# Output stores that go by the less used of two queues, in chunked attention with a token-mixing MLP on one core

## The chip, the core and the metric

The kernel runs on one core of a Trainium2 chip. The metric is device microseconds (us) of one execution; lower is better. Five engines matter: TensorE (PE in the profile: matrix products and transposes), VectorE (DVE), ScalarE (ACT), GpSimd (POOL) and SyncE (SP). SyncE computes nothing: it issues DMA transfers. GpSimd can compute, but here it mostly issues transfers too. The two issue them by different queues, which the profile calls q1, hardware_dynamic (SyncE) and q0, software_dynamic (GpSimd). Both queues feed the same 16 DMA engines of the core.

## The reference

Chunked softmax attention over 8 batches, 8 heads, 576 positions, 64 features, in chunks of 64 positions; then a mixing MLP over the positions of each batch. Cut to what matters:

```python
# attention, each chunk of 64 positions by itself
scores = scale * q_c @ k_c.T
attn = softmax(scores)
out = attn @ v_c                          # then laid out as x[B, S, 512]
# token mixing, per batch
wq = x @ w_q                              # [576, 64]
wk = x @ w_k
W_tok = (1 / sqrt(64)) * wq @ wk.T        # [576, 576]
mixed = W_tok @ x                         # [576, 512]
return relu(mixed) @ w_out                # float32, [8, 576, 512]
```

The output is 8 x 576 x 512 floats, 9.44 MB. It is written to memory once.

## The kernel before, in words

The work is cut into 20 units: for each of the 8 batches two blocks of 256 positions (`m` 0 and 1), and the last 64 positions of the batches, joined in pairs (`m` None). Each unit goes through attention (`attention`), the projections (`project`) and, once a batch has all of its units, the mixing (`mixing`, `mix_out`). W_tok is not formed: the kernel multiplies wk by x first.

The order of all steps is a list written by hand, `ORDER`. A word names a step, an engine (P, V, S for TensorE, VectorE, ScalarE) and a PSUM bank. `Graph.write` walks through it and emits each step. So every engine's instructions, and those of both queues, stand in a fixed order, and an instruction that waits holds up those behind it on its engine.

Loads go by GpSimd's queue, 83 of them, in the order of `LOADS` (the issuing lines L207, L215, L222 and others); between them GpSimd waits for earlier loads to land (`pace`). After the last load (`GATE` = 82 counts from 0) the gate opens (`open_gate`): SyncE waits for the last load's data with a tiny transfer to `gate`, and then the stores held so far are issued. One other kind of transfer goes by SyncE before that: L586 copies half of a tile inside the chip (`wt`).

Stores are made in `mix_out`. TensorE multiplies by w_out (L679), ScalarE or VectorE copies the 128 x 512 result from PSUM into an `osb` buffer (the copy's line is L310, in the helper `copy`), and `ev_o` calls `store`. There are 36 such copies and 24 osb buffers. Four of the buffers are used once more, at the start, for inputs. A copy's data go out in one of two ways:

- whole: 128 rows of 2 KB, 256 KB, one store, by SyncE's queue;
- in halves: two stores of 64 rows, 128 KB each, since the two halves belong to different places of the output. The first goes by SyncE's queue and the second by GpSimd's. In the last batch both halves of an `m` block go by SyncE's.

Up to the gate `store` only notes what to do (`held`); after it, `store` issues at once. `open_gate` issues the held ones at L237, and later ones are issued at L229. In the profiled execution 17 stores are held for SyncE and 9 for GpSimd. After the gate come 19 copies, with 30 stores. In their written order, h for halves and w for whole, they are:

```
h w h w w w h h h h h w h h h w h w w
```

The fourteenth and the fifteenth are of the last batch's `m` blocks, whose halves both go by SyncE. At the program's end (L740) SyncE waits for every store to land, GpSimd runs a DRAIN, and all engines meet in a short handshake.

Of the kernel before, what the change touches and what calls it, by code (L numbers as in the profile page):

```python
# [86 lines left out]
class Graph:  # L87
# [3 lines left out]
    def add(self, kind, u, engines, emit, deps, form="", takes=(), reads=None, size=0, makes=(), uses=()):  # L91
        s = Step(kind, u, engines, emit, deps, form, list(takes), reads, size, list(makes), list(uses))
        self.steps.append(s)
        return s
# [21 lines left out]
def kernel(  # L116
# [10 lines left out]
    nc = tc.nc  # L127
    B, H, S, D = q.shape
# [42 lines left out]
    def ring(shape, dtype, tag):  # L171
        return work.tile(shape, dtype, name=tag, tag=tag, bufs=RINGS[tag])
# [17 lines left out]
    def in_banks(bk, words, dtype=F32):  # L190

        a = ps[:, bk.at : bk.at + bk.n, 0:words]
        return a.bitcast(F16) if dtype == F16 else a

    def half(i):
        return slice(C * i, C * i + C)
# [3 lines left out]
    st, wide, turned, valued = {}, {}, {}, {}  # L200
# [23 lines left out]
    held, moved, QUEUES = [], [], (nc.sync, nc.gpsimd)  # L224

    def store(to, of, queue=nc.sync):

        if "open" in st:
            queue.dma_start(to, of)  # L229
        else:  # L230
            held.append((to, of, queue))

    def open_gate(of):
        nc.sync.dma_start(gate[:], of)
        st["open"] = True
        for to, x, queue in held:
            queue.dma_start(to, x)  # L237

# [33 lines left out]
    for n_load, key in enumerate(LOADS.split()):  # L272
        after, n, last = [], 1024, None
# [12 lines left out]
        elif key[0] == "r":  # L286
            x, part, i = "qkv".index(key[1]), int(key[2]), "ab".index(key[3])
            emit = lambda x=x, part=part, i=i: load_rest(x, part, i)
            n = 512 * (NB2 - 2 if part == 2 else 1)
            last = lambda x=x, part=part, i=i: (v_rest if x == 2 else qkr[:, x])[C * i : C * i + 1, part, 0, 0:1]  # L290
        elif key == "wo":
            emit = lambda: nc.gpsimd.dma_start(wo[:], moe_w_out.rearrange("(f p) n -> p f n", p=P))
            n = 513
            last = lambda: wo[0:1, 0, 0:1]
        else:
            emit = lambda i="qk".index(key[1]): load_w(i, (moe_w_q, moe_w_k)[i])
            n = 512
# [5 lines left out]
        if n_load == GATE:  # L303
            graph.queue.append((lambda last=last: open_gate(last()), lambda: moved))
# [4 lines left out]
    def copy(eng, to, of):  # L309
        (nc.vector.tensor_copy if eng == DVE else nc.scalar.copy)(to, of)  # L310
# [326 lines left out]
    def mix_out(u, batches):  # L637
        b, m = pairs[u]
        ni = 1 if m is None else 2
        toks = ni * P  # L640
        bm = Banks(2)
        rtag = ("ring", f"rm{ni}", u)

        def pe(eng):
            ma = in_banks(bm, 2 * toks).rearrange("p o (f s) -> p o f s", f=2)
            wide = toks // len(batches)

            for f in range(2):
                for i, bb in enumerate(batches):
                    for o in range(2):  # L650
                        s = slice(i * wide, i * wide + wide)
                        nc.tensor.matmul(  # L652
                            ma[:, o, f, s],
                            lhsT=st["g", bb][half(o), f * P : f * P + P],
                            rhs=st["wt", u][half(o), s],
                            start=True,
                            stop=True,
                        )

        def ev(eng):  # L660
            rm = ring([P, NF, toks], F16, f"rm{ni}")
            of = in_banks(bm, 2 * toks)
            to = rm[:].rearrange("p (o f) s -> p o (f s)", o=2)
            if eng == DVE:
                nc.vector.tensor_scalar(to, of, scale_moe, 0.0, op0=ALU.mult, op1=ALU.max)
            else:
                nc.scalar.activation(to, of, AF.Relu, scale=scale_moe)  # L667
            st["rm", u] = rm

        uses = [("ring", f"wt{ni}", u)] + [("ring", "g16", bb) for bb in batches]  # L670
        n = add(f"mix{ni}", u, PE, pe, [n for bb in batches for n in st["g_n", bb]] + [st["wq_n", u]], ROWS, [bm], size=4 * len(batches), uses=uses)
        n = add(f"rm{ni}", u, EITHER, ev, [n], reads=bm, makes=[rtag])
        for i in range(ni):
            bo = Banks(1)

            def pe_o(eng, i=i, bo=bo):
                for f in range(NF):
                    rm = st["rm", u]
                    nc.tensor.matmul(  # L679
                        in_banks(bo, DM)[:, 0],  # L680
                        lhsT=rm[:, f, i * P : i * P + P],
                        rhs=wo[:, f, :],
                        start=(f == 0),
                        stop=(f == NF - 1),
                    )

            def ev_o(eng, i=i, bo=bo):
                osb = ring([P, DM], F32, "osb")
                copy(eng, osb[:], in_banks(bo, DM)[:, 0])
                if m is None:  # L690
                    for c in range(2):
                        store(out[batches[c], S - C : S, :], osb[half(c), :], QUEUES[c])
                elif i == 0:
                    store(out[b, 2 * P * m : 2 * P * m + P, :], osb[:])
                else:

                    for c in range(2):
                        x = 4 * m + 2 + c
                        queue = QUEUES[c if b < B - 1 else 0]
                        store(out[b, x * C : x * C + C, :], osb[half(1 - c), :], queue)  # L700

            n1 = add("out", u, PE, pe_o, [n], FULL, [bo], size=4, uses=[rtag, ("load", "wo")])
            add("osb" if ni == 2 and i == 0 else "osbr", u, EITHER, ev_o, [n1], reads=bo, makes=[("ring", "osb", (u, i))])

    for u, (b, m) in enumerate(pairs):
# [39 lines left out]
```

## Time and profile before

| | |
|---|---|
| median of three runs | 135.4 us (134.92 to 135.56) |
| the profiled execution's own time | 134.47 us |
| its span, first to last instruction | 132.7 us |
| TensorE busy | 120.8 us (91%) |
| VectorE busy | 103.1 us (78%) |
| ScalarE busy | 98.7 us (74%) |
| GpSimd busy | 86.1 us (65%) |
| moved by DMA | 25.54 MB, mean 193 GB/s |
| stores by SyncE | 16 of 256 KB, 22 of 128 KB, median 3.7 us from issue to landing |
| stores by GpSimd | 18 of 128 KB, median 4.0 us from issue to landing |

How to read it: all times inside the profile are us from the span's start, and the profiled execution's own time holds 1.8 us more than the span. A store has two parts: its issue, which takes time on SyncE or GpSimd, and the time until it has landed. The profile's list of busy engines doesn't count SyncE's issuing, so SyncE's queue is read from the timeline. `SPq` and `POOLq` mark an engine's queue instructions. The rows that the prediction rests on are shown there.

### The profile page before, as it was taken

The numbers are of one execution on the slowest core, as the hardware profiler recorded it, in microseconds if no ns is written. First come the engines' busy times: TensorE is split into PE (matmuls) and PEld (weight loads), VectorE is DVE, ScalarE is ACT, GpSimd is POOL, SyncE is SP. The second block draws the span as 40 slices with busy tenths as digits, with TensorE's granted clock in tenths as the row PEclk, the third lists the DMA queues.
The fourth block names the chain that finished last, engine by engine and source line by source line (L and its number), as shares of the span: only waits on it lengthen the run. The fifth ranks groups of instructions, "written<-read, shape, count | busy, mean of one in ns | idle before, by whom it ended". The sixth has DMA issues, their size and how long they took to land.

```text
span 132.7 us, 5277 instructions
## 1 busy us (share of the span) xinstructions
PE 120.8 (91%) x2225; PEld 81.7 (62%) x2225; DVE 103.1 (78%) x197; ACT 98.7 (74%) x185; POOL 86.1 (65%) x138
## 2 busy tenths in 40 slices
PE   5999799989999999999999999999999999999700
PEld 2465577665577758777859686677666665644200
DVE  6235899997779999979999899999988976574200
ACT  3554574649979998898979969979979978756500
POOL 7999799963899946875976897799663003121100
PEclk9999999999999999999999999999999999999995
DMA  3999999999999999999999999999999999998892
GB/s 108 244 159 165 167 160 164 177 198 159 172 167 164 158 149 136 167 146 162 172 170 150 172 163 162 180 182 162 174 303 271 295 267 306 238 316 259 229 303 104
DMA packets 86906, 25.54 MB, mean 193 GB/s; under 512 B 79586, under 2 KB 82850, under 8 KB 86882
## 3 DMA queue, kind: packets, MB, share of 16 engines
q0 software_dynamic: 79504, 16.65, 144.2%
q1 hardware_dynamic: 7378, 8.56, 21.0%
q8 instruction: 17, 0.28, 0.8%
q14 instruction: 7, 0.06, 0.1%
HBM read 29.62 MB, written 9.44 MB: 294 GB/s over the span
## 4 chain that ended last, share of the span: by engine, by line
PE 57%; DMA 14%; POOL 9%; DVE 7%; ACT 4%; issue 3%; POOLq 0%
PE ps L679 22%; DMA qk<-in_q_dram 9%; PE ps L380 6%; PE ps L465 5%; DMA qkr<-in_k_dram 5%; PE ps L420 4%; PE ps L555 4%; PE ps L545 4%; PE ps L652 3%; PE ps L498 3%; POOL qk L207 3%; POOL v_all L215 2%; PE ps L614 2%; DVE mx L433 2%; POOL qkr L222 2%
## 5 line engine op out<-in xcount | busy, mean ns | idle before, releaser
L679 PE MATMUL ps<-wo,rm 128*128 128x512 f16 x144 | 35.9, 380 | 0.3 <-ACT osb L310 0.2
L215 POOL DMA_DIRECT2D v_all<-in_v_dram x32 | 28.4, 900 | 0.0
L433 DVE TENSOR_REDUCE mx<-ps 128x16 f32<-128x1024 f32 (+1 forms) x20 | 22.2, 1111 | 5.3 <-PE ps L406 3.7
L525 DVE TENSOR_TENSOR xs<-ps,rec 128x512 f16<-128x512 f32 x36 | 23.8, 685 | 0.4
L380 PE MATMUL ps<-ident,qk 128*64 128x128 f16 x512 | 20.8, 225 | 0.7 <-DMA qk<-in_q_dram 0.5
L453 ACT ACTIVATE es<-sh 128x1024 f16<-128x1024 f32 (+1 forms) x20 | 19.5, 977 | 0.7 <-DVE sh L441 0.3
L443 DVE TENSOR_TENSOR sh<-ps,mx 128x1024 f32<-128x1024 f32 x16 | 19.6, 1224 | 0.4
L679 PEld LDWEIGHTS <-rm 128*128 128x128 f16 x144 | 12.3, 98 | 12.3 <-issue 1.2
L380 PEld LDWEIGHTS <-qk 128*64 128x64 f16 x512 | 15.7, 111 | 4.6 <-DMA qk<-in_q_dram 1.0
L310 ACT COPY osb<-ps 128x512 f32<-128x512 f32 x29 | 16.4, 590 | 2.7 <-PE ps L679 2.5
L229 POOL DMA_DIRECT2D out_dram<-osb x9 | 4.8, 529 | 21.0 <-ACT osb L310 15.0
L310 ACT COPY qbd<-ps 64x512 f32<-64x512 f32 (+1 forms) x27 | 14.6, 539 | 3.7 <-PE ps L364 2.1
L667 ACT ACTIVATE rm<-ps 128x1024 f16<-128x1024 f32 (+1 forms) x15 | 14.0, 946 | 2.3 <-PE ps L652 1.8
L207 POOL DMA_DIRECT2D qk<-in_k_dram x15 | 13.2, 881 | 3.2 <-issue 2.2
L207 POOL DMA_DIRECT2D qk<-in_q_dram x15 | 13.4, 894 | 2.3 <-PE ps L420 0.7
L310 ACT COPY xt<-ps 128x512 f32<-128x512 f32 (+1 forms) x16 | 8.9, 554 | 4.0 <-DVE rec L515 1.7
L545 PE MATMUL ps<-ident,xs 128*128 128x128 f16 x144 | 11.4, 219 | 0.4 <-DVE xs L525 0.4
L712 PE MATMUL ps<-ones 128*128 128x512 f16 (+1 forms) x45 | 10.3, 357 | 1.5 <-DVE ones L188 1.5
L555 PE MATMUL ps<-xt,wqk 128*128 128x256 f16 (+1 forms) x80 | 11.0, 262 | 0.5 <-ACT xt L310 0.5
L310 ACT COPY et<-ps 128x512 f32<-128x512 f32 (+1 forms) x17 | 9.2, 541 | 2.4 <-PE ps L465 1.3
L310 ACT COPY kt<-ps 128x512 f32<-128x512 f32 (+1 forms) x14 | 7.8, 556 | 4.2 <-PE ps L380 4.2
L465 PEld LDWEIGHTS <-es 128*128 128x128 f16 x144 | 8.9, 98 | 3.0 <-ACT es L453 1.9
(69 smaller groups left out, 190.2 us busy)
## 6 DMA issues: line engine op xcount, KB each, us to landing
v_all<-in_v_dram POOLq DMA_DIRECT2D x32, 128.0 KB, 6.3
out_dram<-osb SPq DMA_DIRECT2D x16, 256.0 KB, 3.7
qk<-in_q_dram POOLq DMA_DIRECT2D x15, 256.0 KB, 6.3
qk<-in_k_dram POOLq DMA_DIRECT2D x15, 256.0 KB, 6.4
out_dram<-osb SPq DMA_DIRECT2D x22, 128.0 KB, 3.7
out_dram<-osb POOLq DMA_DIRECT2D x18, 128.0 KB, 4.0
osb<-in_q_dram SPq DMA_DIRECT2D x2, 256.0 KB, 3.2
osb<-in_k_dram SPq DMA_DIRECT2D x2, 256.0 KB, 3.9
```

The costliest lines, as they stand in the source:

```text
L207: nc.gpsimd.dma_start(qk[u][:, t], rows_of((q, k)[t], u))
L215: nc.gpsimd.dma_start(v_home(u, i)[:, :, 0:D], of)
L310: (nc.vector.tensor_copy if eng == DVE else nc.scalar.copy)(to, of)
L380: nc.tensor.transpose(tp[half(o), j, :, r, :], of, ident[:])
L433: nc.vector.tensor_reduce(mx[:], scores(), axis=AX.X, op=ALU.max)
L443: nc.vector.tensor_tensor(out=sh[:].rearrange("p x (g r) -> p x r g", r=R), in0=in_banks(bs, 512).rearrange("p i (x r g) -> p (i x) r g", ...
L453: nc.scalar.activation(es[:].rearrange("p x s -> p (x s)"), st["sh", u][:].rearrange("p x s -> p (x s)"), AF.Exp, scale=scale_attn,)
L465: nc.tensor.transpose(ep[:, x, :], es[:, x, :], (ident if m is None else order)[:])
L525: nc.vector.tensor_tensor(out=to, in0=xp()[:, :, :, 0:D], in1=by, op=ALU.mult)
L545: nc.tensor.transpose(tx[:, f, i, :], xs[u][:, i, 2 * f : 2 * f + 2, :], ident[:])
L555: nc.tensor.matmul(pj, lhsT=wqk[:, f].rearrange("p i j -> p (i j)"), rhs=st["xt", u][:, f, :], start=(f == 0), stop=(f == NF - 1),)
L679: nc.tensor.matmul(in_banks(bo, DM)[:, 0], lhsT=rm[:, f, i * P : i * P + P], rhs=wo[:, f, :], start=(f == 0), stop=(f == NF - 1),)
```

## The change

`store` no longer uses the queue that its caller names, once the gate is open. It keeps two counts, `st["open"]`, one for SyncE's queue and one for GpSimd's. A store goes by SyncE's queue if its count is not above GpSimd's, and otherwise by GpSimd's, and the count of the queue that it took goes up by one. At the gate SyncE's count is set to the number of stores held for SyncE, and GpSimd's to 0. The size of a store does not enter. Held stores go by the queue that was noted for them. In `ev_o` the exception for the last batch is dropped, so that its second half names GpSimd's queue; after the gate the name has no effect.

```diff
     def store(to, of, queue=nc.sync):
         if "open" in st:
-            queue.dma_start(to, of)
+            n = 0 if st["open"][0] <= st["open"][1] else 1
+            QUEUES[n].dma_start(to, of)
+            st["open"][n] += 1
         else:
             held.append((to, of, queue))
 
     def open_gate(of):
         nc.sync.dma_start(gate[:], of)
-        st["open"] = True
+        st["open"] = [sum(x[2] is nc.sync for x in held), 0]
         for to, x, queue in held:
             queue.dma_start(to, x)
...
                     for c in range(2):
                         x = 4 * m + 2 + c
-                        queue = QUEUES[c if b < B - 1 else 0]
+                        queue = QUEUES[c]
                         store(out[b, x * C : x * C + C, :], osb[half(1 - c), :], queue)
```

## The prediction

> **What bounds the kernel now.** I read the page first, then the timelines of SyncE's queue (SP) and GpSimd (POOL) after the loads, then the copies that make the stores' data, then the end of the program, and last what the DMA engines do meanwhile.
>
> From the page, the span and the DMA engines' busy tenths in 40 slices of 3.3 us; then, from the timelines, the last load that GpSimd issues and SyncE's two runs of stores (start, length, line, count):
>
> ```profile
> span 132.7 us, 5277 instructions
> DMA  3999999999999999999999999999999999998892
> ...
> 90.53 1.76 POOL L215 DMA_DIRECT2D v_all<-in_v_dram  x2
> ...
> 98.49 13.08 SPq L237 DMA_DIRECT2D out_dram<-osb  x17
> 111.67 16.75 SPq L229 DMA_DIRECT2D out_dram<-osb  x21
> ```
>
> SyncE issues stores without a pause from 98.49 to 128.42: first the 17 that were held (L237), then the 21 that came up after the gate (L229). The same two lines, by source, with the duration of one issue (min/median/max, ns) and where they lie; the fifth row is the page's group of GpSimd's later stores, with its idle time:
>
> ```profile
> L237 SPq DMA_DIRECT2D out_dram<-osb x17: 362/595/1343, 98.5 to 111.1; - x17
> L237 POOL DMA_DIRECT2D out_dram<-osb x9: 529/529/582, 92.3 to 98.8; - x9
> L229 SPq DMA_DIRECT2D out_dram<-osb x21: 414/551/1753, 111.7 to 128.0; - x21
> L229 POOL DMA_DIRECT2D out_dram<-osb x9: 529/529/529, 100.7 to 124.6; - x9
> ...
> L229 POOL DMA_DIRECT2D out_dram<-osb x9 | 4.8, 529 | 21.0 <-ACT osb L310 15.0
> ```
>
> GpSimd, with nine of the later stores, is idle for 21.0 us among them, 15.0 of it until ScalarE has made the next copy. SyncE is never idle. How far behind the data it is, the timeline of the end shows:
>
> ```profile
> 119.15 6.22 PE L679 MATMUL ps<-wo,rm 128*128 128x512 f16 x28
> ...
> 123.68 0.59 ACT L310 COPY osb<-ps 128x512 f32<-128x512 f32 x1 [1.14 <-PE ps L679]
> 124.54 0.59 ACT L310 COPY osb<-ps 128x512 f32<-128x512 f32 x1 [0.28 <-PE ps L679]
> 124.55 0.53 POOL L229 DMA_DIRECT2D out_dram<-osb  x1 [2.75 <-ACT osb L310]
> 125.40 0.59 ACT L310 COPY osb<-ps 128x512 f32<-128x512 f32 x1 [0.28 <-PE ps L679]
> ```
>
> TensorE ends at 125.4 and the last copy at 126.0. GpSimd issues its half of the copy that ends at 124.27 at 124.55, 0.28 us behind. SyncE issues the store of the last copy at 128.0, 2.0 us behind. What follows that, by line: the last store alone, its landing, the program's closing line L740, and SyncE's waits there:
>
> ```profile
> L229 SPq DMA_DIRECT2D out_dram<-osb x1: 414/414/414, 128.0 to 128.0; - x1
> DMA to landing us min/median/max: 3.4/3.4/3.4
> ...
> L740 SPq EVENT_SEMAPHORE  x11: 17/28/28, 128.5 to 132.6; - x11
> L740 POOLq EVENT_SEMAPHORE  x4: 17/17/17, 131.9 to 132.6; - x4
> L740 POOLq DRAIN  x3: 51/93/4247, 124.5 to 132.4; - x3
> ...
> SPq L740 <- DMA out_dram<-osb: 2.9, 2, 2.3
> ```
>
> The last store lands at 128.0 + 3.4 = 131.4, and the span ends 1.3 us later. So the end is set by a line of stores that is 2.0 us behind its data, not by TensorE. Either SyncE's issuing holds that line back, or the DMA engines do; the forecast hangs on which.
>
> **The change, part by part.** *The counters.* At the gate the counts are [17, 0]: the nine stores held for GpSimd are not counted. GpSimd therefore gets the next 17 stores, whatever they are, and only then do the queues alternate. How many copies come after the gate, on ScalarE and VectorE, and the sizes of SyncE's stores after 111.6, these rows say:
>
> ```profile
> L310 ACT COPY osb<-ps x13: 578/586/603, 99.8 to 125.4; 128x512 f32<-128x512 f32 x13
> L310 DVE COPY osb<-ps x6: 680/681/692, 108.5 to 122.8; 128x512 f32<-128x512 f32 x6
> ...
> out_dram<-osb SPq DMA_DIRECT2D x8, 256.0 KB, 3.6
> out_dram<-osb SPq DMA_DIRECT2D x13, 128.0 KB, 3.6
> ```
>
> So 19 copies: 8 stored whole (256 KB, all on SyncE), 11 as two halves of 128 KB (13 of these on SyncE, 9 on GpSimd). In their written order, which the section on the kernel gives, GpSimd takes the 16 stores of the first ten copies and one half of the eleventh; then SyncE gets the other half and the queues take turns. SyncE ends with 7 (five halves, two whole) where it has 21, GpSimd with 23 (17 halves, six whole) where it has 9. The very last store falls to SyncE, the one before it, a whole one, to GpSimd. The second edit (the last batch's halves on both queues) only names a queue for held stores, and none of that batch is held: nothing.
>
> *Before the gate* nothing changes: the held stores, the loads and the copies of L586 keep queue and order. GpSimd's last load is issued at 90.5 to 92.3, so no load stands behind the stores that it gains.
>
> *GpSimd's issuing.* A half costs 0.53 us (x9, all 529). A whole one by GpSimd is not in the trace: not under 0.53, and not over the dearest load that GpSimd issues, in whose row one of 128 KB in 1024 pieces takes 0.90:
>
> ```profile
> L215 POOL DMA_DIRECT2D v_all<-in_v_dram x32 | 28.4, 900 | 0.0
> ```
>
> A whole store has 128 rows where a half has 64, so I take 0.6. The sum is 17 x 0.53 + 6 x 0.6 = 12.6 us (12.2 to 14.4) in the 25 us from 100.4 to 125.4: room enough. The waits for copies move to GpSimd's queue, with nothing behind them but later stores.
>
> *SyncE's issuing.* The 17 held ones still take 13 us or more, beside a busier GpSimd. Even 5 us more, to 117, is hidden: its first later store has its data only at the eleventh copy, the first of these two:
>
> ```profile
> 117.97 1.28 DVE L310 COPY osb<-ps 128x512 f32<-128x512 f32 x2
> ```
>
> That is about 118.6. Buffers: osb has 24, so the last copy, at 125.4, needs the buffer of the twelfth held copy, whose store is issued before the last held one at 111.1: even 5 us later it is in time.
>
> *The end.* SyncE's last store then has nothing ahead of it: it goes at about 126.2 in place of 128.0. To land, the store of that size issued at 126.2 took 2.7 and the last one 3.4. GpSimd's last goes at 125.13 + 0.28 = 125.4; its nine took 2.9 to 4.6:
>
> ```profile
> L229 SPq DMA_DIRECT2D out_dram<-osb x1: 536/536/536, 126.2 to 126.2; - x1
> DMA to landing us min/median/max: 2.7/2.7/2.7
> ...
> L229 POOL DMA_DIRECT2D out_dram<-osb x9: 529/529/529, 100.7 to 124.6; - x9
> DMA to landing us min/median/max: 2.9/3.9/4.6
> ```
>
> So SyncE's last lands at 128.9 to 129.6 (I take 129.2) and GpSimd's at 128.3 to 130.0 (129.1). By SyncE's side the span is 129.2 + 1.3 = 130.5. By GpSimd's, its DRAIN counts: it now lasts from 124.5 to 128.8, some 1.3 us past the landing of GpSimd's last store (124.55 + 2.9), and hides behind SyncE's last landing. Moved, it ends between 125.4 + 4.25 = 129.7 and 130.0 + 1.3 = 131.3; with 129.1, at 130.4. The closing handshake after it (131.9 to 132.6 now) adds 0.7: 131.1. I take the later of the two, 131.1, a gain of 1.6 us.
>
> *The DMA engines' time.* The stores' bytes stay, but 2,560 KB (2.62 MB: six whole, eight halves) change from the hardware queue q1 to the software queue q0. Shares of the engines by stage, and by queue from 99.5 to the end:
>
> ```profile
> 106.00:111.50 5.50, 5.47 (x111) 3.55 (x110) 4.01 (x15) 4.57 (x11) 0.00 (x0) 1.00 0.91 282
> 111.50:118.00 6.50, 6.26 (x62) 3.69 (x61) 3.77 (x7) 4.70 (x11) 2.11 (x4) 1.00 0.92 272
> 118.00:125.50 7.50, 7.37 (x47) 3.25 (x44) 3.67 (x6) 4.06 (x7) 1.59 (x3) 1.00 0.88 262
> ...
> q1 hardware_dynamic: 4064, 7.08, 66.8%
> q0 software_dynamic: 533, 1.45, 18.6%
> ```
>
> The last two columns of a stage are the DMA share and GB/s. Over 33.2 us, q1 used 22.2 us of all 16 engines for 7.08 MB, 3.1 us per MB; q0 6.2 us for 1.45 MB, 4.3 per MB. Together 28.4 of the 31.9 us up to the last landing: 3.5 us idle. So the engines are nearly full, and the price of a MB on q0 matters. It varies; here are q0's rows while single GpSimd stores moved, in the windows 126.1 to 126.9 and 122.6 to 124.8:
>
> ```profile
> q0 software_dynamic: 47, 0.13, 42.0%
> ...
> q0 software_dynamic: 48, 0.13, 39.1%
> ```
>
> 0.42 x 0.8 us for 0.13 MB is 2.6 us per MB; 0.391 x 2.2 us is 6.6. By the low price the move saves 2.62 x (3.1 - 2.6) = 1.3 us of engine time; by the mean price it costs 2.62 x (4.3 - 3.1) = 3.1; the 6.6 is one store. I take 3.4, nearer the low end, because a packet's time in these rows includes waiting beside SyncE's packets, and SyncE has a third of its later stores left: 0.8 us more, 29.2 in all. From 99.5 that is 128.7 with no idle engine: level with the landings above, so issuing and data set the end. The sum stays -1.6.
>
> The Trainium skill (DMA: Bandwidth & Descriptors, "Issuing engines are not separate DMA queues") says the opposite of a gain in bandwidth: DMAs from any issuer share the same 16 engines, and several issuers only save issue time. By that rule the sum would be near 0. The 0.91 with SyncE alone (106 to 111.5) speaks for it, the 0.88 where SyncE has mostly halves to issue (118 to 125.5) less so.
>
> **In numbers.** The profiled execution took 134.47 us, 0.93 below the median of 135.4; I subtract 1.6 from both: 132.9 and 133.8.
>
> **Rivals.** *The engines are full.* At q0's mean price of 4.3 the engines alone need 28.4 + 3.1 = 31.5 us from 99.5, to 131.0 against 131.4 now: a gain of 0.4 at most, 135.0. This is what the rule above would give. For it: DMA tenths of 9 up to the end. Against: 3.5 us idle. The same time comes out if GpSimd's DRAIN ends at 131.3 (132.0 span) and a little more.
>
> *Software packets make the drain of stores slower.* The mean price holds and the engines still idle as now, since idling comes from bursts of copies and not from SyncE: +3.1, 138.5; half of that, 136.9. It decides above 3.1 + 0.7/2.62 = 3.4 us per MB if no idle time is won back. For it: 6.6 in the one window; q0's mean. Against: 2.6 in the other, and a line of stores that is behind on SyncE alone while GpSimd waits.
>
> *The counters don't balance*: they leave GpSimd with 23 of 30. That is in the sum.
>
> **How the numbers follow.** Forecast 0.53: 132.6 (a gain of 2.8, SyncE's 128.9 with no DRAIN in the way, 130.2, and a little from cheaper packets) to 134.7. Full engines or the DRAIN 0.20: 134.7 to 136.0. Slower 0.27: 136.1 to 138.5, two thirds of it below 136.9. The range 132.6 to 136.9 leaves out some 0.09 above and 0.04 below. About 0.5% (0.7 us) is what a measurement of this kernel can tell from no change: faster 0.53, same 0.20, slower 0.27.
>
> **What would show it.** Right: seven stores at L229 on SyncE, with a pause before 118.7; 23 on GpSimd, none much over 0.6 us; the last store issued within 0.4 us of the last copy's end; a span near 131. Wrong: landings over 4.5 us for GpSimd's last stores, a lower GB/s at the same DMA share from 100 to 118 (dear packets), a DRAIN that ends last, or a TensorE end later than 125.4.

## The result, and the profile after

The changed kernel takes 134.07 us (median of 20 runs, 131.85 to 136.10); the kernel before, run beside it, 135.34 (20 runs, 133.03 to 138.40). The ratio is 0.9883, with a 95% interval of 0.9836 to 0.9931: faster by 1.2%. 133.8 was forecast where the median was 135.4, a fall of 1.6 us; the medians fell by 1.3 us (0.9906 of before), and the ratio, on 135.34, says 1.6.

Ratios here and below compare only the fast runs, those within 1.5% of each kernel's fastest (here 9 of 20 on either side), so they are not the ratios of the medians, and the one profile of the changed kernel that belongs to this result is of a slower run, whose loads ended 2.8 us later than in the profile of before. A second profile of the same kernel (a1_after, below) stands beside it. L231 and L240 are now what L229 and L237 were, L313 is the copy and L743 the end.

From the page, the span and the DMA tenths; from the timeline, SyncE's two runs; then the stores by line (issue time min/median/max in ns, first and last start in us):

```profile
span 133.6 us, 5273 instructions
DMA  3999999999999999999999999999997999999992
...
101.30 19.94 SPq L240 DMA_DIRECT2D out_dram<-osb  x17
121.33 7.41 SPq L231 DMA_DIRECT2D out_dram<-osb  x7
...
L240 SPq DMA_DIRECT2D out_dram<-osb x17: 359/1048/2083, 101.3 to 119.8; - x17
L231 SPq DMA_DIRECT2D out_dram<-osb x7: 403/467/992, 121.3 to 128.3; - x7
L231 POOL DMA_DIRECT2D out_dram<-osb x23: 529/529/593, 103.0 to 127.7; - x23
```

The counts are 7 and 23. GpSimd's six whole stores cost hardly more to issue than the halves: no issue is over 0.593 us. SyncE's 17 held stores take 19.9 us, where they took 13.1. Their median issue went from 595 to 1048 ns, although SyncE does nothing else: something that SyncE feeds seems to push back, which b1_half_before tests. The end, in the timeline (the last copy) and by source (GpSimd's last store, its landing, SyncE's last store, and the closing line):

```profile
127.73 0.59 ACT L313 COPY osb<-ps 128x512 f32<-128x512 f32 x1 [0.28 <-PE ps L682]
...
L231 POOL DMA_DIRECT2D out_dram<-osb x1: 577/577/577, 127.7 to 127.7; - x1
...
DMA to landing us min/median/max: 4.2/4.2/4.2
...
L231 SPq DMA_DIRECT2D out_dram<-osb x1: 403/403/403, 128.3 to 128.3; - x1
...
L743 SPq EVENT_SEMAPHORE  x4: 28/28/28, 132.4 to 132.6; - x4
L743 POOLq DRAIN  x1: 5129/5129/5129, 127.7 to 127.7; - x1
```

The copy ends at 128.32 and SyncE issues its store at once (128.3), not 2.0 us later. But the store lands late: SyncE gets past its wait for it at 132.4, 4.1 us after the issue, where the last one took 3.4 before. GpSimd's last lands after 4.2 us, and its DRAIN ends at 127.73 + 5.13 = 132.9, just after SyncE's last waits. From the end of the last copy to the end of the span it is 133.6 - 128.3 = 5.3 us; before it was 132.7 - 126.0 = 6.7. At the end of the last copy 1.36 MB had still to move before, and 1.01 MB now.

What the DMA engines did, by stage (the last two columns are DMA share and GB/s); the first five rows are of the kernel before, the last four of the changed one:

```profile
100.00:106.00 6.00, 6.00 (x103) 3.76 (x101) 5.42 (x10) 5.75 (x10) 1.06 (x2) 1.00 0.97 288
106.00:112.00 6.00, 5.73 (x113) 3.65 (x112) 4.51 (x15) 5.07 (x13) 0.46 (x1) 1.00 0.90 285
112.00:118.00 6.00, 6.00 (x61) 3.59 (x60) 3.27 (x7) 4.20 (x10) 1.64 (x4) 1.00 0.92 269
118.00:126.00 8.00, 7.37 (x47) 3.25 (x44) 3.67 (x6) 4.55 (x7) 1.59 (x3) 1.00 0.88 258
126.00:128.00 2.00, 0.00 (x0) 0.00 (x0) 0.00 (x0) 0.00 (x0) 0.00 (x0) 1.00 0.97 310
...
101.00:106.00 5.00, 5.00 (x76) 2.81 (x75) 4.42 (x9) 4.71 (x8) 3.74 (x8) 1.00 0.84 219
106.00:112.00 6.00, 6.00 (x93) 3.86 (x92) 4.97 (x11) 5.17 (x10) 1.30 (x3) 1.00 0.99 312
112.00:118.00 6.00, 5.73 (x94) 3.81 (x94) 3.85 (x9) 4.98 (x12) 3.52 (x7) 1.00 0.96 299
118.00:126.00 8.00, 8.00 (x60) 3.77 (x59) 4.93 (x8) 4.25 (x8) 3.75 (x7) 1.00 0.96 291
```

From 106 to 126 the same engines move 9 to 13% more per us, at a share of 0.96 to 0.99 in place of 0.88 to 0.92. These are the rows that show it best. The changed kernel's gate is 2.8 us later here; from the first held store to the last copy the mean is 286 GB/s (101.3 to 128.3) where it was 271 (98.5 to 126.0), 5% more. And SyncE's queue with little beside it can fill the engines: in the kernel before they stand at 0.97 up to 106, and at 0.97 with 310 GB/s after 126, when GpSimd has issued its last store. (The share adds up the times of packets, which can overlap: it reads 1.98 from 90 to 94 in the changed kernel's profile. The GB/s are the safer column.) So the first reading is that with two queues the DMA engines are filled better between 106 and 126, not that one queue can't fill them. The experiments ask whether it was SyncE's issuing or the engines that held the line back, and which part of the change matters.

### The profile page after: what moved, and what is told of

Same layout as the page of the kernel before. It is cut to its first block, busy times and chain, and to the rows that moved or that the text cites. A ratio compares the mean times of both kernels' runs of the same rounds, so it can differ in the third digit from the quotient of the medians.

```text
span 133.6 us, 5273 instructions
## 1 busy us (share of the span) xinstructions
PE 121.6 (91%) x2225; PEld 81.7 (61%) x2225; DVE 103.2 (77%) x197; ACT 99.1 (74%) x185; POOL 93.7 (70%) x152
## 4 chain that ended last, share of the span: by engine, by line
PE 40%; DMA 21%; POOL 12%; DVE 9%; issue 7%; ACT 5%; POOLq 1%; DVEq 0%
DMA v_all<-in_v_dram 16%; PE ps L682 11%; PE ps L715 6%; DMA qk<-in_q_dram 5%; PE ps L383 4%; POOL qk L207 4%; POOL v_all L215 4%; PE ps L468 3%; POOL out_dram L231 3%; PE ps L558 3%; PE ps L548 3%; PE ps L423 3%; DVE mx L436 2%; PE ps L655 2%; DVE sh L446 2%
## 5 line engine op out<-in xcount | busy, mean ns | idle before, releaser
L231 POOL DMA_DIRECT2D out_dram<-osb x23 | 12.4, 541 | 13.8 <-DVE osb L313 7.8
L313 ACT COPY osb<-ps 128x512 f32<-128x512 f32 x29 | 16.4, 590 | 2.9 <-PE ps L682 1.7
L313 ACT COPY qbd<-ps 64x512 f32<-64x512 f32 (+1 forms) x27 | 14.6, 540 | 3.9 <-PE ps L383 1.8
L715 PE MATMUL ps<-ones 128*128 128x512 f16 (+1 forms) x45 | 11.0, 377 | 1.5 <-DVE ones L188 1.5
L313 ACT COPY xt<-ps 128x512 f32<-128x512 f32 (+1 forms) x16 | 8.9, 555 | 4.0 <-DVE rec L518 1.7
L313 ACT COPY et<-ps 128x512 f32<-128x512 f32 (+1 forms) x17 | 9.2, 540 | 2.8 <-PE ps L468 1.6
L313 ACT COPY kt<-ps 128x512 f32<-128x512 f32 (+1 forms) x14 | 7.8, 556 | 4.2 <-PE ps L383 4.1
```

Of the source, the lines that this page charges most:

```text
L231: QUEUES[n].dma_start(to, of)
L715: nc.tensor.matmul(ps[:, i, 0:cols], lhsT=ones[:, 0:P], rhs=ones[:, 0:cols], start=True, stop=True)
```

## The experiments

Each ratio is to the kernel before, run in turn on the same chip. "Lag" is from the end of the last copy to the issue of SyncE's last store, "tail" from the end of the last copy to the end of the span. Lag and tail are of one profile each.

| kernel | median, us | median of the kernel before beside it | ratio (95% interval) | lag, us | tail, us |
|---|---|---|---|---|---|
| before (first profile) | 135.34 | | | 2.0 | 6.7 |
| c0_before | 134.83 | 134.75 | 1.0041 (0.9992 to 1.0091) | 2.8 | 7.4 |
| changed (first profile) | 134.07 | 135.34 | 0.9883 (0.9836 to 0.9931) | 0.0 | 5.3 |
| a1_after | 133.31 | 134.63 | 0.9958 (0.9924 to 0.9991) | 0.0 | 5.3 |
| a2_last_batch | 134.41 | 134.63 | 0.9998 (0.9939 to 1.0058) | 1.8 | 5.5 |
| a3_from_zero | 133.43 | 134.63 | 0.9904 (0.9847 to 0.9962) | GpSimd's: 0.3 | 5.8 |
| b3_sync_last | 133.63 | 134.63 | 1.0001 (0.9966 to 1.0037) | 2.5 | 6.8 |
| a4_all_pool | 134.39 | 134.67 | 0.9975 (0.9932 to 1.0017) | GpSimd's: 0.6 | 6.9 |
| b1_half_before | 130.50 | 134.67 | 0.9688 (0.9635 to 0.9741) | 0.0 | 3.0 |
| b2_half_after | 131.06 | 134.67 | 0.9736 (0.9664 to 0.9808) | 0.0 | 3.2 |
| c2_whole | 133.14 | 134.75 | 0.9910 (0.9870 to 0.9950) | 0.0 | 4.4 |
| c1_gate_early | 132.84 | 134.75 | 0.9890 (0.9827 to 0.9953) | 0.0 | 5.1 |
| d2_early_end | 133.24 | 135.10 | 0.9872 (0.9815 to 0.9928) | 0.0 | 5.7 |
| b4_act | 150.71 | 134.67 | 1.1062 (1.0955 to 1.1168) | 0.0 | 4.5 |

**a1_after: the changed kernel again.** No edit.

> The changed kernel again, for a second profile and a ratio. Theory (SyncE's line of stores was behind its data): the last store is issued within 0.1 us of the last copy's end, where it was 2.0 us behind; from the gate's first SyncE store to the end of the span about 32.3 us, 34.2 before; ratio to before 0.985 to 0.993. Rival (the DMA engines set the end, the two queues only fill their gaps): the same lag at issue, but landings grow by 1 us or more and take back half of it; the DMA share after the gate is 0.95 or more in every stretch.

Lag and tail came out as in the first profile (0.0 and 5.3), and the last landings again took about 4 us. From SyncE's first held store (97.2) to the end it was 34.6 us, not 32.3: here the loads ended 4 us earlier, and the stores had caught up with the copies before the end, as its stages show:

```profile
112.00:118.00 6.00, 5.76 (x61) 3.39 (x58) 3.45 (x6) 4.72 (x11) 3.40 (x7) 1.00 0.98 310
118.00:122.00 4.00, 4.00 (x33) 1.99 (x32) 3.35 (x5) 2.01 (x4) 2.03 (x5) 1.00 0.76 228
```

The engines are full up to 118 and at 0.76 after it: they wait for copies. So the 0.95 "in every stretch" that the rival named did not hold here; in this execution the copies and the time that the last stores take set the end. The ratio of these runs, 0.9958, is less of a gain than 0.9883 and than the 0.985 to 0.993 expected; the two intervals just overlap (0.9924 to 0.9931), and the medians differ by 1.3 us both times.

**c0_before: the kernel before again.** No edit.

> The kernel before once more, for a second profile and to see how far the ratio of one kernel to itself strays. If the 2.0 us by which SyncE's last store trailed its copy is the kernel's and not one execution's, the last store is again issued 1.2 us or more behind and the span ends 6 to 7 us after the last copy. Ratio 0.996 to 1.004.

```profile
111.54 17.60 SPq L229 DMA_DIRECT2D out_dram<-osb  x21
...
125.35 0.59 ACT L310 COPY osb<-ps 128x512 f32<-128x512 f32 x1 [0.28 <-PE ps L679]
```

The copy ends at 125.9; SyncE's last store, the last of a run that ends at 129.1, is issued 2.8 us behind it; tail 7.4, over the 6 to 7 expected. The lag is the kernel's. A kernel against itself gave 1.0041, at the edge of what was expected, so a difference of 0.4% in the table is not to be built on.

**b1_half_before and b2_half_after: half of the bytes, as many stores.** These runs ask whether SyncE's issuing alone makes the line. The held stores are halved in the same way, and so are those of b2_half_after; a store has as many rows as before, of 1 KB in place of 2 KB.

```diff
-            queue.dma_start(to, of)
+            queue.dma_start(to[:, 0:256], of[:, 0:256])
```

> The kernel before with every store cut to its first 256 of 512 columns: as many stores, by the same queues, half of the bytes (the other half of the output is left out). Theory (SyncE's own issuing is the line): an issue on SyncE stays near its mean of 0.79 us from the gate on, the 38 of them take about 30 us, and the last store is still about 2 us behind the last copy. Rival (the DMA engines push back on SyncE's issuing): with half of the bytes the mean falls to 0.5 us or less, the line ends with the last copy and the last store is issued within 0.3 us of it; the span ends 4.5 us or less after the last copy, 6.7 before.

> The changed kernel with every store cut to its first 256 of 512 columns (half of the output is left out). If, with the change, the engines' backlog is what is left at the end: the last landings fall from 4 us or more to about 2.5, and the span ends about 4 us after the last copy, 5.3 with whole rows. If what is left is the fixed time of a store and of GpSimd's DRAIN: 5.0 us or more still.

SyncE's two runs in b1_half_before, and their issue times:

```profile
98.11 10.36 SPq L237 DMA_DIRECT2D out_dram<-osb  x17
108.56 17.23 SPq L229 DMA_DIRECT2D out_dram<-osb  x21
...
L237 SPq DMA_DIRECT2D out_dram<-osb x17: 355/577/1073, 98.1 to 108.0; - x17
L229 SPq DMA_DIRECT2D out_dram<-osb x21: 380/500/587, 108.6 to 125.4; - x21
...
SPq L229 <- DVE osb L310: 4.8, 3, 2.4
```

The same 38 issues on one queue: the held ones take 10.4 us in place of 13.1, no later one is over 0.59 us (1.75 before), SyncE now waits for copies (4.8 us for VectorE's alone), and the last store goes out with its copy. The rival was right in the main: added up over the trace, the 38 issues take 20.1 us, where with all bytes they take 26.8, in some 27.5 us from the first held store to the last copy. The mean of 0.53 us is a little above the 0.5 that the rival named. So SyncE's own issuing is most of its time and does not make the line by itself; what the bytes add does. With half of them the change brings nothing: 3.0 and 3.2 us of tail, 0.9688 and 0.9736. In the changed kernel, too, it is bytes that are left and not a fixed time: its tail falls from 5.3 to 3.2, and the last landings from about 4 us to about 2. That they are a backlog isn't shown: a1_after, whose stores had caught up, has the same 5.3 as the first profile, so it may be the bytes of the last stores alone.

**a2_last_batch: only the last batch's halves on two queues.**

```diff
-                        queue = QUEUES[c if b < B - 1 else 0]
+                        queue = QUEUES[c]
```

> The kernel before, with only the second halves of the last batch's two m blocks by GpSimd's queue; no counters. SyncE has 19 later stores, not 21. Theory: two issues of 0.6 to 0.7 us leave SyncE's line near its end, so the last store is 0.6 to 0.8 us behind its copy, not 2.0, and the time falls by 0.9 to 1.3 us (ratio 0.991 to 0.994), most of what the whole change gives. Rival (engines full): the bytes and the engines' load stay, the time moves by 0.3 us at most (0.998 to 1.002).

The lag of 1.8 us is 0.3 and 1.1 below the two profiles of the kernel before, not 1.2 to 1.4 below the first: two issues fewer buy less than their issue time. The time didn't move (0.9998), as the rival said; but its interval reaches from -0.6% to +0.6%, and its one tail of 5.5 us speaks for some gain: inconclusive.

**a3_from_zero: counters that start equal.**

```diff
-        st["open"] = [sum(x[2] is nc.sync for x in held), 0]
+        st["open"] = [0, 0]
```

> The changed kernel with both counters starting from 0 at the gate: plain alternation, 15 later stores each, 17 more held ones for SyncE. Theory: SyncE has six issues fewer than before, at 0.78 us some 4.7 us, more than the 2.0 us that it was behind, so the last store is again issued within 0.3 us of its copy and the time is that of the changed kernel within 0.3%. Rival (what matters is that GpSimd takes the first 17 beside SyncE's held ones, so that the engines are fed by two queues from the gate on): half or less of the gain, ratio 0.994 to 1.0.

```profile
106.00:112.00 6.00, 5.73 (x113) 3.55 (x110) 4.54 (x14) 5.06 (x13) 1.23 (x3) 1.00 0.89 290
112.00:118.00 6.00, 6.00 (x61) 3.50 (x59) 3.29 (x6) 3.98 (x9) 1.43 (x3) 1.00 0.95 280
118.00:126.00 8.00, 7.15 (x46) 3.25 (x44) 3.46 (x5) 4.55 (x7) 3.21 (x6) 1.00 0.92 278
```

0.9904, tail 5.8, and a median 0.1 us from a1_after's beside it: the gain is there without giving GpSimd the first 17. What is needed is that both queues have stores up to the end. The engines are hardly fuller than in the kernel before (0.89 to 0.95 with 278 to 290 GB/s), so the gain does not hang on shares of 0.96 to 0.99.

**b3_sync_last and a4_all_pool: one queue alone at the end.**

```diff
-            n = 0 if st["open"][0] <= st["open"][1] else 1
+            n = 0 if st["open"][0] <= st["open"][1] or sum(st["open"]) >= 34 else 1   # b3_sync_last
+            n = 1                                                                     # a4_all_pool
```

> The changed kernel, but after GpSimd's first 17 later stores all the remaining 13 go by SyncE. GpSimd is done near 119, so its DRAIN can't end last. Theory: 13 issues of 0.55 to 0.75 us take 7.2 to 9.8 us for 7.4 us of copies, so SyncE is behind by 0 to 2 us again; slower than the changed kernel by 0.3 to 1.3 us. Rival (GpSimd's DRAIN, which ended last in the changed kernel's profile, is what is left at the end): faster than the changed kernel by about 0.5 us.

> The changed kernel with all 30 later stores by GpSimd's queue; SyncE has its 17 held ones only. Theory: GpSimd's issues of 0.53 to 0.58 us, 30 of them, take 17 us of 25, so no line forms; the last store is issued 0.3 us after its copy and the end is set by its landing (4 us) and GpSimd's DRAIN, 5.3 to 6.0 us after the last copy; time within 0.5% of the changed kernel. Rival (software packets cost the engines more, 4.2 us per MB against 3.1): 1.3 MB more by that queue costs 1.4 us; 6.5 us or more from the last copy to the end, slower than the changed kernel by 1%.

First the timeline and the stage of b3_sync_last (SyncE alone after 118), then those of a4_all_pool (GpSimd alone):

```profile
118.24 10.00 SPq L231 DMA_DIRECT2D out_dram<-osb  x13
118.00:126.00 8.00, 6.75 (x44) 3.06 (x40) 3.05 (x5) 4.55 (x7) 0.53 (x1) 1.00 0.89 250
...
121.81 5.85 POOL L231 DMA_DIRECT2D out_dram<-osb  x11 [0.72 <-DVE osb L313]
122.00:126.00 4.00, 3.89 (x19) 1.56 (x16) 0.69 (x1) 2.02 (x5) 4.00 (x8) 1.00 0.84 230
```

With either queue alone a line forms behind the copies (2.5 us on SyncE, 0.6 on GpSimd, issuing 11 stores without a pause) and the tail is that of the kernel before, 6.8 and 6.9. In b3_sync_last the 13 stores took 10.0 us for 7.4 us of copies, a little more than the theory's 7.2 to 9.8, and GpSimd's DRAIN had nothing to do with it: GpSimd's last store had gone at 118.3. What the line cost there is less sure: the ratio, 1.0001, says the whole gain, but by the medians b3_sync_last is 0.3 us above a1_after and 1.0 below the kernel before, both run beside it. In a4_all_pool, where ratio and medians agree that nearly all of the gain is gone, I expected no line, and was wrong; the mean price of a MB on the software queue did not rise as the rival had it (3.5 us of all 16 engines, not 4.2), but the tail did, and GpSimd's DRAIN ended last, at 132.6, 0.9 us after SyncE's last wait. The DMA engines stand at 0.89 and 0.84, although stores are waiting from 118 and from 122 on.

**c2_whole: one 128-row store for two halves.**

```diff
-                    for c in range(2):
-                        x = 4 * m + 2 + c
-                        queue = QUEUES[c]
-                        store(out[b, x * C : x * C + C, :], osb[half(1 - c), :], queue)
+                    x = 4 * m + 2
+                    store(out[b, x * C : x * C + 2 * C, :], osb[:])
```

> The changed kernel with the two halves of an m block's second copy stored as one 128-row store (which writes the two 64-row chunks in swapped places). Bytes the same, 38 stores in all of 128 rows in place of the pairs, and those of the rests in halves as before. If issuing is what matters: SyncE's held line is no shorter in stores but the later ones are 8 or 9 fewer; little to win over the changed kernel, within 0.3%. If the engines are what matters and a half, read from half of the partitions, is dear: q0 and q1 together need 1 us or more less for the bytes after the gate than the 28 us of the changed kernel, and the span ends 0.5 us or more earlier after the last copy.

From 100.2 to 131.2, the two queues (packets, MB, share of 16 engines):

```profile
q1 hardware_dynamic: 2730, 4.94, 46.2%
q0 software_dynamic: 1360, 4.33, 41.2%
```

Of 31.0 us, q1 used 14.3 for 4.94 MB and q0 12.8 for 4.33: 2.9 and 2.95 us per MB, against 3.1 and 3.4 in the changed kernel. So a half looks dearer to the engines than half of a whole store, and the tail falls by 0.9 us, to 4.4. The engines' side was right here, though the 27.1 us of both queues are only 0.6 and 0.9 below the changed kernel's 27.7 and 28.0, and the time shows no gain over it (0.9910 against 0.9883 and 0.9958). (There were 40 stores in all, 8 of them halves, not the 38 that I wrote.)

**c1_gate_early and d2_early_end: toward a faster one.** SyncE's held stores wait for an earlier load; in d2_early_end the last two stores, too, go by SyncE.

```diff
-            graph.queue.append((lambda last=last: open_gate(last()), lambda: moved))
+            graph.queue.append((lambda: open_gate(v_home(17, 1)[0:1, 0, 0:1]), lambda: moved))
...
-            n = 0 if st["open"][0] <= st["open"][1] else 1
+            n = 0 if st["open"][0] <= st["open"][1] or sum(st["open"]) >= 45 else 1   # d2_early_end only
```

> The changed kernel with SyncE's gate waiting for the load of v that is third from last instead of the last one, so that SyncE's held stores start about 3 us earlier, beside the last three loads. If the engines' queue of bytes after the gate is what is left at the end: faster than the changed kernel by 0.5 to 1.5 us. If the last loads come later by as much (they carry TensorE's last chain): the last copy comes up to 1 us later and nothing is won or something lost.

> The changed kernel with the early gate of c1_gate_early, and its last two stores (both whole) by SyncE, so that GpSimd's last store is a half some 0.9 us earlier. If GpSimd's DRAIN, which ends 0.9 to 1.3 us after the landing of its last store, is the last thing in the early-gate kernel: the DRAIN ends near 129.5 and SyncE's last landing takes over, 0.3 to 0.6 us less from the last copy to the end (4.5 to 4.8, where it was 5.1), ratio to before 0.984 to 0.988. If the landing of the last bytes sets it by whichever queue: 5.0 us or more, ratio 0.988 to 0.991.

In c1_gate_early the gate's transfer went at 93.3, 2.7 us before the last load landed (96.0) and 4.4 us earlier than in the first profile of the kernel before, and the last copy ended at 126.0, as there: the last loads didn't suffer. The tail is 5.1, hardly below the changed kernel's, since there, too, the stores have caught up before the end when the loads end early. The ratios, 0.9890 and 0.9872, are at the level of the changed kernel's first one; the medians, 132.84 and 133.24, are 0.5 and 0.1 below that of a1_after, from other sessions. Whether they beat the changed kernel stays open. In d2_early_end the DRAIN began with GpSimd's last store and took 5.07 us:

```profile
L743 POOLq DRAIN  x3: 51/102/5070, 124.0 to 130.8; - x3
```

It ended at 129.1, and SyncE's side, whose last store landed at 129.5, took over, as the theory had it. But the tail of 5.7 is against the theory: moving GpSimd's last store forward did not shorten the end. Both sides end at nearly the same time in the changed kernel, and to bring one forward wins nothing when the other gets one whole store more.

**b4_act: ScalarE's queue in place of GpSimd's.**

```diff
-            QUEUES[n].dma_start(to, of)
+            (nc.sync, nc.scalar)[n].dma_start(to, of)
```

> The changed kernel with its later stores divided in the same way between SyncE's queue and ScalarE's, none by GpSimd: no software packets after the held ones and no store of GpSimd's before its DRAIN. If packets or the DRAIN of GpSimd's queue are what limits the changed kernel, this is faster by 0.5 us or more. Against that, ScalarE issues 23 stores itself, at 0.05 to 0.6 us each, between its copies, and waits for VectorE's copies in order: if an issue costs ScalarE 0.5 us the last copies come 2 us later or more and it is slower than the changed kernel by 1% or more. I expect the second.

```profile
L231 ACTq DMA_DIRECT2D out_dram<-osb x23: 338/497/1295, 104.3 to 144.0; - x23
ACT osb L313 <- DMA out_dram<-osb: 6.0, 2, 4.2
```

23 issues of 0.5 us and the waits that come with them stand between ScalarE's copies; the last copy ends at 145.0, 19 us later. The loss was expected, its size wasn't. It says nothing about packets.

## Why the prediction was right, point by point

*SyncE's line is behind its data and the change ends that*: shown. The lag is 2.0 and 2.8 us in two profiles of the kernel before, 0.0 in two of the changed one, and comes back with one queue at the end (b3_sync_last). The tail went from 6.7 and 7.4 to 5.3 both times.

*The counters, 7 and 23; 0.6 us for a whole store by GpSimd*: as forecast; at most 0.593 us.

*The held stores are hidden even 5 us longer*: true by a hair. They took 19.9 us, 6.9 longer, and ended at 121.2 (17.2 us in a1_after, where they ended at 114.5, with room to spare); the first later store of SyncE went at 121.33, with its copy (the first of the two below) done at about 121.0:

```profile
120.30 1.28 DVE L313 COPY osb<-ps 128x512 f32<-128x512 f32 x2
```

*The landing*: mis-sized. I gave SyncE's last store 2.7 to 3.4 us and it took 4.1; GpSimd's last, 2.9 to 4.6 and taken as 3.7, took 4.2. With half of the bytes they took 1.8 and 2.1 (b2_half_after), so it is bytes that they wait for: in the changed kernel two whole stores end together on two queues. That is some 0.7 us of the tail.

*The DRAIN*: the sum had it end 5.0 us after GpSimd's last issue (125.4 to 130.4) and last of all by 0.6 us; it lasted 5.1 and ended last, but by no more than 0.2 us in both profiles of the changed kernel. That the tail came out so near, 131.1 - 126.0 = 5.1 forecast and 5.3 measured, is in part luck: GpSimd's landing was 0.5 us longer than I took, its DRAIN ended 0.9 us after the landing and not 1.3, and SyncE's side, too short by 0.7, was hidden behind them. I also listed a DRAIN that ends last as a sign of being wrong, though my own sum had it so.

*TensorE's end*: an end later than 125.4 was a sign of being wrong, and it came (127.7, and 125.9 in a1_after). The change is hardly its cause: with an earlier gate or other counters, and as many stores by two queues, TensorE ended at 125.3 and 125.2 (c1_gate_early, a3_from_zero).

*The price of a MB on the software queue*: I took 3.4, between 2.6 and 4.3. These are q0 and q1 in the changed kernel from 102.3 to 133.6, and in a1_after from 98.2 to 131.9:

```profile
q0 software_dynamic: 1399, 4.07, 44.7%
q1 hardware_dynamic: 2560, 4.46, 43.9%
...
q1 hardware_dynamic: 2560, 4.46, 43.1%
q0 software_dynamic: 1407, 4.10, 39.9%
```

0.447 x 31.3 us for 4.07 MB is 3.4 us per MB, and 0.399 x 33.7 for 4.10 is 3.3. So the slower rival's condition, the mean price of 4.3, was not met, and its line of 3.4 was met only just. Its other condition, that no idle time is won back, failed in the first profile (286 GB/s for 271).

*The rival "the engines are full"*: half right, and the text posed the alternative wrongly. I set "SyncE's issuing" against "the engines"; b1_half_before shows that both go into the line: 20.1 of the 26.8 us of issuing stay with half of the bytes, and the rest is the engines' answer. Yet the engines were not full: from 106 to 126 they moved 258 to 285 GB/s before and 291 to 312 after. By the rule of the Trainium skill (DMA: Bandwidth & Descriptors, "Issuing engines are not separate DMA queues"), several issuers only save issue time. The runs don't refute that, since the kernel before reached 0.97 and 310 GB/s after GpSimd's last issue and a3_from_zero gained at 278 to 290; what they show is that the saving was worth 1.2% here, where I took the rule to mean a sum near 0. Why the engines stood at 0.88 to 0.92 from 106 to 126 isn't settled. One cause was not tested: from 118 to 126 most of SyncE's stores are halves, and 128 KB each 0.55 us, its median issue, is about 240 GB/s (an estimate), less than the engines moved elsewhere.

*The size*: 1.6 us forecast, 1.3 by the medians of both sessions. That there is less to win in executions whose loads end early, since the stores then catch up by themselves, fits a1_after but isn't shown: no such profile of the kernel before was compared.

## What to carry to other kernels

When stores are behind at the end, ask by halving the bytes at the same number of issues whether the issuer alone holds them; here the 38 issues with half of the bytes made no line. A line behind its data on one queue, beside a second queue with idle time, was worth 1.2% even though both feed the same 16 engines, and plain alternation did it as well as the counters. What has to be shared out is the stores of the last 10 us: one queue alone there brought the line and the long tail back, whichever it was (what it cost in time is sure for GpSimd alone, and between 0.3 us and the whole gain for SyncE), while who took the first 17 made no difference that could be measured.

## What the runs showed of the hardware

Issue time on SyncE is no constant: the same 17 held stores had a median of 577, 595, 891 and 1048 ns with half the bytes, with all, and beside a busier GpSimd queue in the two profiles of the changed kernel. GpSimd's issue of a later store stayed at 527 to 622 ns in every profile, for 64 and for 128 rows alike, with the engines at 0.99. And stores of 64 rows seem dearer to the engines than halves of one of 128: 3.1 and 3.4 us of all 16 engines per MB in the changed kernel's first profile, where 40 of 56 stores are halves, and 2.9 and 2.95 in c2_whole, where 8 of 40 are.
